# A streamed weight unit fetched by two transfers of 64 partitions in place of one of 128

## The chip, the cores and the metric

The kernel runs on one core of one Trainium2 chip. The metric is the device time of one execution in microseconds, as the median of several runs. The profile is one more execution, recorded by the hardware profiler.

## The reference

The reference adds three things to each other: the input `x`, a two-layer network with GELU on the normalised input (`B`), and an attention layer that carries a memory from segment to segment (`A`). Only `A` matters for the change:

```python
xn = layernorm(x)                      # 2048 x 1024
mem = mem0                             # 8 x 1024
for s in range(64):                    # segments of 32 rows, strictly one after the other
    h = concatenate([mem, xn[32*s : 32*s + 32]])          # 40 x 1024
    q, k, v = h @ Wq, h @ Wk, h @ Wv                      # 32 heads of 128: each W is 1024 x 4096
    p = softmax(where(mask, q @ k.T / sqrt(128), -1e9))   # per head, 40 x 40
    o = (p @ v) @ Wo                                      # Wo is 4096 x 1024
    mem = o[:8];  outs.append(o[8:])
return x + concatenate(outs) + gelu(xn @ w1 + b1) @ w2 + b2
```

The memory that segment s leaves is an input of segment s + 1, so the 64 segments can't be computed side by side. Each of them needs all four weight matrices, 32 MB in bf16[...].

## The kernel before, in words

**Two stages.** The first stage (lines 270 to 548) computes the layer norm and the GELU network for all rows in four groups, and puts rows to be added later into DRAM. The second (from line 555) is the loop over the 64 segments.

**Units, resident and streamed.** The four matrices are cut into 64 units of 512 KB, each a tile of 128 partitions by 2,048 bf16 values, 4 KB in a partition. `ORDER` (line 67) is the order in which a segment uses them: K, Q, K, Q, V, V, then the 16 units of the output product. Forty-six units are fetched once and stay in SBUF for the whole loop. The 18 others, marked `S` in the hand-written string `PLACED` (line 68), are *streamed*: they are fetched again in every segment from copies that stand contiguously in DRAM (`copies`, line 192, named `Wc_...` in the profile). One of the 18 (`IN_PSUM`) is kept in PSUM after the first segment and is brought back by VectorE copies (lines 224 to 226), so later segments fetch 17. One of these (`HALF`) has half of its columns resident and is fetched as 256 KB.

**The ring.** `start_stream` (line 220) begins the fetch of the next streamed unit into one of six buffers (`STREAM_BUFS`), in rotation, from the SyncE queue (line 229). It is called six times at the end of the first stage (line 516) and after that by `unit_done` (line 608), each time a streamed unit has been used. So a new fetch waits until TensorE has done with the unit that held the same buffer six units ago. All fetches are issued by SyncE in program order; a waiting one holds up those behind it. In the segment loop SyncE issues next to nothing else; the small loads and stores of rows go through GpSimd's queue.

**Who uses the units.** `half_pass` (line 668) goes over the eight units of half of K, Q or V and calls `product` (line 644), which runs four 32-column-wide matmuls of 512 values at line 650. `o_product` (line 820) does the same for the output product, at line 829. Both take streamed tiles from a queue in the order in which they were begun (`unit_tile`, line 596). Small steps of attention (`scores`, `sums`, `values`) are placed between units.

**Completion.** The framework gives the transfers of the hardware queue eight semaphores in rotation. A transfer that is given a semaphore waits for the transfer that had it before, the eighth back.

Of the kernel before, what the change touches and what calls it, by code (L numbers as in the profile page):

```python
# [78 lines left out]
def kernel(  # L79
# [16 lines left out]
    nc = tc.nc  # L96
# [42 lines left out]
    def slab(place):  # L139
        if place in low:  # L140
            return low[place]
        return slabs.tile([P, 2048], BF16, name="u", tag=place)
# [9 lines left out]
    for j in range(4):  # L152
# [10 lines left out]
        out=m, in_=m, pattern=[[1, NX]], compare_op=ALU.is_ge, fill=0.0, base=0, channel_multiplier=-1,  # L163
    )
    for half in range(2):
        m = mask_left[0:SEG, :, 8 - 8 * half:16 - 8 * half]
        nc.gpsimd.affine_select(
            out=m, in_=m, pattern=[[-8, GRP], [0, 8]], compare_op=ALU.is_ge, fill=0.0, base=0, channel_multiplier=1,
        )
        nc.gpsimd.affine_select(  # L170
            out=m, in_=m, pattern=[[8, GRP], [1 if half else 0, 8]], compare_op=ALU.is_ge, fill=0.0,
# [13 lines left out]
    for k in range(7):  # L185
# [6 lines left out]
    copies = {  # L192
        unit: dram.tile([P, 1024 if unit == HALF else 2048], BF16, name="Wc_" + "_".join(map(str, unit)))[:, :]
        for unit in reversed(ORDER) if IS_STREAMED[unit]
    }
# [20 lines left out]
    streams = [unit for _ in range(NSEG) for unit in ORDER if IS_STREAMED[unit]]  # L216
    stream_tiles = deque()
    started = 0

    def start_stream():  # L220
        nonlocal started
        if started < len(streams):
            t = slab(RING[started % STREAM_BUFS])
            if streams[started] == IN_PSUM and "kept" in nxt:
                for b in range(2):
                    nc.vector.tensor_copy(out=t[:, 1024 * b:1024 * b + 1024], in_=nxt["kept"][:, b, :])  # L226
            else:
                c0 = 1024 if streams[started] == HALF else 0
                nc.sync.dma_start(out=t[:, c0:2048], in_=copies[streams[started]])
            stream_tiles.append(t)  # L230
            started += 1

# [38 lines left out]
    with tc.tile_pool(name="ma", bufs=2) as ma, tc.tile_pool(name="mps", bufs=6, space=PSUM) as mps:  # L271
# [28 lines left out]
        for j in range(4):  # L300
            nc.sync.dma_start(
                out=o_sb[32 * j + NX:32 * j + 32, 0:8, :],
                in_=mem0[:, 256 * j:256 * j + 256].rearrange("m (h e) -> m h e", h=8),
# [6 lines left out]
        for i in range(14):  # L310
            t = slab(f"w2_{i}")[:, :].rearrange("p (c d) -> p c d", d=DM)
# [120 lines left out]
        for tg in range(4):  # L432
# [14 lines left out]
            for fb in range(FC):  # L447
                ps = mps.tile([P, 512], F32, name="ps")
                for kt in range(KT):
# [9 lines left out]
                    out=xb[:, :], in_=ps[:, :], func=ACT.Identity, bias=b1col[:, fb:fb + 1], scale=1.0  # L459
# [4 lines left out]
                    out=u[:, :], in0=u[:, :], scalar1=0.044715, scalar2=1.0, op0=ALU.mult, op1=ALU.add  # L464
# [7 lines left out]
            if tg == 0:  # L472
                for nb in range(2):
                    cs = slice(nb * 512, nb * 512 + 512)
                    ps = mps.tile([P, 512], F32, name="ps")
# [3 lines left out]
            if not last:  # L479
# [10 lines left out]
                for t in range(4):  # L490
# [3 lines left out]
                    for nb in range(2):  # L494
                        cs = slice(nb * 512, (nb + 1) * 512)
                        ps = mps.tile([P, 512], F32, name="ps")
# [16 lines left out]
            else:  # L513


                for _ in range(STREAM_BUFS):
                    start_stream()
# [37 lines left out]
    with tc.tile_pool(name="late", bufs=1) as late, \  # L555
# [40 lines left out]
        def unit_tile(unit):  # L596
            if IS_STREAMED[unit]:
                return stream_tiles.popleft()[:, :]
            return res_tiles[unit]
# [8 lines left out]
        def unit_done(unit):  # L608

            if IS_STREAMED[unit]:  # L610
                start_stream()
                if late_units:
                    fetch_late(late_units.popleft())
                for _ in range(2 if len(small) > 8 else 1):
                    if small:
                        small.popleft()()
# [9 lines left out]
        for s in range(NSEG):  # L626
# [269 lines left out]
            for n, unit in enumerate(O_UNITS):  # L896
                t = unit_tile(unit)
# [26 lines left out]
            for w, r in enumerate(tiles):  # L924
                nc.vector.tensor_tensor(out=r[:, :], in0=psX[:, 256 * w:256 * w + 256], in1=r[:, :], op=ALU.add)  # L925
                if left_o and not final:

                    for b in range(2):
                        c0 = 256 * (2 * b + w)
# [71 lines left out]
```

## Time and profile before

| What | Value |
|---|---|
| median of 3 runs | 1974.53 us (1971.98 to 1985.32) |
| profiled span | 1971.6 us |
| PE busy | 1771.2 us, 90% |
| VectorE, ScalarE, GpSimd busy | 855.1, 591.9, 287.0 us |
| data moved by DMA | 644.36 MB, mean 327 GB/s |
| streamed transfers (line 229) | 1,025 of 512 KB, 64 of 256 KB |
| first streamed fetch | at 363.4 us |
| last streamed fetch begun | at 1958.2 us |

The page has a row of 40 slices of the span for each engine, with its busy share in tenths, and below them the share for the core's 16 DMA engines and their rate in GB/s. A stretch is the same for a window of one's own choice: length, busy time of each engine with its number of instructions, then the granted TensorE clock, the DMA share and the rate. A line of the waits reads: engine, line of the waiting instruction, what it waited for, then the sum in us, the number of waits and the longest one. A piece of the chain reads: start, length, and what ran or was waited for. PE busy time has to be read with care here: the ends of matmuls are modelled[...].

### The profile page before, as it was taken

How to read it: one execution, taken by the hardware profiler on the slowest of the kernel's cores; microseconds unless marked ns; L12 is line 12 of the kernel's file. 1: busy time of each engine (PE TensorE's matmuls, PEld its weight loads, DVE VectorE, ACT ScalarE, POOL GpSimd, SP SyncE). 2: the span in 40 equal slices, each digit the busy share in tenths (PEclk: the TensorE clock that was granted, in tenths of full speed). 3: DMA queues.
4: the chain of work that ended last, by engine and by line, in shares of the span. 5: the costliest groups of instructions: out<-in, count | busy, mean ns of one | idle time of the engine just before them, and what ended most of it. 6: DMA issues, size and time to landing. Idle time of an engine off the chain costs nothing.

```text
span 1971.6 us, 77130 instructions
## 1 busy us (share of the span) xinstructions
PE 1771.2 (90%) x34271; PEld 962.3 (49%) x34291; DVE 855.1 (43%) x2233; ACT 591.9 (30%) x1349; POOL 287.0 (15%) x557
## 2 busy tenths in 40 slices
PE   6999999999888989898889888989888988998887
PEld 3444444445444445555444546555455454554544
DVE  6657575414344334344434443434344443434432
ACT  4434343302222223222223222222222322222222
POOL 0000000002331111111112111211111111111112
PEclk9999999999999999999999999999999999999999
DMA  9821212689999999999999999999999999999998
GB/s 335 264 56 42 57 41 56 247 305 390 376 363 383 368 372 384 364 379 369 382 371 390 380 392 367 388 377 385 358 386 371 391 379 379 374 389 377 388 367 331
DMA packets 225850, 644.36 MB, mean 327 GB/s; under 512 B 48123, under 2 KB 61739, under 8 KB 225500
## 3 DMA queue, kind: packets, MB, share of 16 engines
q1 hardware_dynamic: 207228, 619.26, 83.7%
q0 software_dynamic: 16928, 18.77, 2.9%
q8 instruction: 268, 4.39, 0.9%
q10 hardware_dynamic: 1360, 1.39, 0.2%
q14 instruction: 66, 0.54, 0.1%
HBM read 625.08 MB, written 31.26 MB: 333 GB/s over the span
## 4 chain that ended last, share of the span: by engine, by line
PE 63%; DMA 26%; issue 5%; DVE 4%; ACT 1%; POOL 1%; ACTq 0%; POOLq 0%; DVEq 0%
PE acc L650 28%; DMA u<-Wc_O 12%; PE acc L829 10%; PE ps L450 10%; PE ps L498 7%; DMA u<-Wc_V 7%; DMA u<-Wc_Q 4%; DMA out_dram<-res 2%; PE ps L531 2%; PE mixed L803 1%; DVE b_oL L707 1%; PE mixed L753 1%; PE acc L803 1%; POOL out_dram L963 1%; PE pT L531 1%
## 5 line engine op out<-in xcount | busy, mean ns | idle before, releaser
L650 PE MATMUL acc<-u,hr 128*32 128x512 bf16 x11520 | 791.9, 382 | 33.3 <-DMA u<-Wc_V 12.1
L650 PEld LDWEIGHTS <-hr 128*32 128x32 bf16 x12288 | 351.6, 97 | 313.9 <-issue 72.5
L650 PE MATMUL acc<-u,hrL 128*32 128x512 bf16 x2880 | 260.7, 389 | 6.1 <-issue 5.9
L829 PE MATMUL acc<-u,d_oL 128*32 128x256 bf16 (+1 forms) x3330 | 184.2, 292 | 20.4 <-issue 11.1
L450 PE MATMUL ps<-u 128*128 128x512 bf16 x896 | 196.2, 382 | 2.6 <-ACT u L346 2.6
L829 PE MATMUL acc<-u,b_oL 128*32 128x256 bf16 (+1 forms) x1776 | 127.1, 304 | 51.3 <-DMA u<-Wc_O 32.1
L829 PEld LDWEIGHTS <-b_oL 128*32 128x32 bf16 (+1 forms) x3552 | 115.5, 102 | 109.6 <-issue 76.2
L498 PE MATMUL ps<-u 128*128 128x512 bf16 x657 | 146.2, 379 | 0.8
L450 PEld LDWEIGHTS <-u 128*128 128x128 bf16 x896 | 88.2, 98 | 109.4 <-issue 5.5
L829 PEld LDWEIGHTS <-d_oL 128*32 128x32 bf16 (+1 forms) x3552 | 100.6, 98 | 62.0 <-issue 34.4
L650 PEld LDWEIGHTS <-hrL 128*32 128x32 bf16 x3072 | 91.8, 98 | 63.7 <-issue 24.4
L829 PE MATMUL acc<-W_O,b_oL 128*32 128x256 bf16 (+1 forms) x1776 | 112.8, 302 | 7.3 <-issue 7.3
L879 POOL DMA_DIRECT2D res<-hr_d x64 | 35.8, 559 | 559.7 <-DVE d_oL L816 304.1
L707 DVE STREAM_TRANSPOSE kT<-kT 128x512 bf16<-128x512 bf16 x64 | 45.5, 711 | 164.4 <-ACT kT L693 164.4
L226 DVE COPY u<-kept 128x1024 bf16<-128x1024 bf16 x126 | 81.2, 687 | 77.7 <-PE acc L829 60.0
L803 PEld LDWEIGHTS <-v 32*128 32x128 bf16 x2048 | 63.6, 91 | 97.8 <-issue 74.5
L707 DVE STREAM_TRANSPOSE b_oL<-b_oL 128x512 bf16<-128x512 bf16 x128 | 90.6, 708 | 46.8 <-ACT b_oL L693 46.8
L693 ACT CAST kT<-acc 128x512 bf16<-128x512 f32 x64 | 37.5, 586 | 222.0 <-PE acc L650 222.0
L498 PEld LDWEIGHTS <-u 128*128 128x128 bf16 x672 | 65.3, 98 | 77.3 <-DVE g_u L466 0.4
L693 ACT CAST b_oL<-acc 128x512 bf16<-128x512 f32 x128 | 75.4, 589 | 80.2 <-PE acc L650 80.2
L963 POOL DMA_DIRECT2D out_dram<-res x124 | 63.4, 517 | 246.5 <-DVE res L925 245.9
L816 DVE CAST b_oL<-acc 128x160 bf16<-128x160 f32 x128 | 41.6, 325 | 131.7 <-PE acc L809 131.7
(139 smaller groups left out, 2221.8 us busy)
## 6 DMA issues: line engine op xcount, KB each, us to landing
u<-Wc_O SPq DMA_DIRECT2D x320, 512.0 KB
u<-Wc_K SPq DMA_DIRECT2D x256, 512.0 KB
u<-Wc_V SPq DMA_DIRECT2D x256, 512.0 KB
u<-Wc_Q SPq DMA_DIRECT2D x193, 512.0 KB
u<-Wc_O SPq DMA_DIRECT2D x64, 256.0 KB
u<-in_B_w_dram SPq DMA_DIRECT2D x16, 448.0 KB
u<-in_B_w_dram SPq DMA_DIRECT2D x14, 512.0 KB
u<-in_A_Wq_dram SPq DMA_DIRECT2D x12, 512.0 KB
```

The costliest lines, as they stand in the source:

```text
L226: nc.vector.tensor_copy(out=t[:, 1024 * b:1024 * b + 1024], in_=nxt["kept"][:, b, :])
L450: nc.tensor.matmul(ps[:, :].rearrange("p (s t) -> p s t", t=SEG), lhsT=w1_sb[fb // 14 * 8 + kt][:, (fb % 14) * P:(fb % 14 + 1) * P], rhs=x ...
L498: nc.tensor.matmul(ps[:, :], lhsT=gts[fc // 4][:, fc % 4, t * P:(t + 1) * P], rhs=w2_sb[fc // 2][:, fc % 2, cs], start=(fc == 0), stop=(fc ...
L531: nc.tensor.matmul(pss[2 * t + nb][:, :], lhsT=gts[fc // 4][:, fc % 4, t * P:(t + 1) * P], rhs=w2_sb[fc // 2][:, fc % 2, nb * 512:nb * 512 ...
L650: nc.tensor.matmul(o, lhsT=lhs[:, i, :], rhs=m, start=(i == seq[0]), stop=(i == seq[-1]), tile_position=(0, 32 * j),)
L693: cp(out=out, in_=ps.rearrange("p (h e) -> p h e", e=32))
L707: nc.vector.transpose(out=home, in_=home)
L803: nc.tensor.matmul(oV[b][:, c, :], lhsT=V[q, c * P:(c + 1) * P], rhs=prA[q, c, :], start=(c == 0), stop=False, skip_group_check=True, tile ...
L816: cp(out=outs[u][:, hs, NL * slot:NL * slot + 40], in_=oV[b])
L829: nc.tensor.matmul(acc[r:r + n // 8, 0:n], lhsT=lhs[:, 4 * (i % 4) + 2 * u + k, :], rhs=w_k[:, n * jq:n * jq + n], start=(unit == O_UNITS[ ...
L879: nc.gpsimd.dma_start(out=st["res"][:, :], in_=hr_d[s + 1, :, 256:512])
L963: nc.gpsimd.dma_start(out=out_flat[rows, 256 * j:256 * j + 256], in_=res[32 * j:32 * j + NX, :])
```

## The change

Each streamed fetch is begun as two transfers, one for partitions 0 to 63 and one for partitions 64 to 127, one behind the other on the same queue, in place of one for all 128. Bytes, source, destination and order stay as they are. Its purpose is to have smaller transfers, each with a completion of its own, for the same unit. The other fetches (resident units, rows, the first stage's weights) are untouched.

```diff
             else:
                 c0 = 1024 if streams[started] == HALF else 0
-                nc.sync.dma_start(out=t[:, c0:2048], in_=copies[streams[started]])
+                for b in range(2):
+                    ps = slice(64 * b, 64 * b + 64)
+                    nc.sync.dma_start(out=t[ps, c0:2048], in_=copies[streams[started]][ps, :])
             stream_tiles.append(t)
             started += 1
```

## The prediction

> **What bounds the kernel now.** I read the page from the top, then the table of stretches, the waits of the transfer queue, the chain in a window, and the compiled instruction order of both kernels. The page first, because it misleads:
>
> ```profile
> PE 1771.2 (90%) x34271; PEld 962.3 (49%) x34291; DVE 855.1 (43%) x2233; ACT 591.9 (30%) x1349; POOL 287.0 (15%) x557
> ...
> DMA  9821212689999999999999999999999999999998
> GB/s 335 264 56 42 57 41 56 247 305 390 376 363 383 368 372 384 364 379 369 382 371 390 380 392 367 388 377 385 358 386 371 391 379 379 374 389 377 388 367 331
> ...
> q1 hardware_dynamic: 207228, 619.26, 83.7%
> ...
> PE 63%; DMA 26%; issue 5%; DVE 4%; ACT 1%; POOL 1%; ACTq 0%; POOLq 0%; DVEq 0%
> PE acc L650 28%; DMA u<-Wc_O 12%; PE acc L829 10%; PE ps L450 10%; PE ps L498 7%; DMA u<-Wc_V 7%; DMA u<-Wc_Q 4%; DMA out_dram<-res 2%; PE ps L531 2%; PE mixed L803 1%; DVE b_oL L707 1%; PE mixed L753 1%; PE acc L803 1%; POOL out_dram L963 1%; PE pT L531 1%
> ```
>
> TensorE looks like the bound at 90% and 63% of the chain. But the DMA row sits at 9 (90% or more) in every slice from the tenth to the last but one. The stretches say how full it really is; the last columns are clock, DMA share and GB/s:
>
> ```profile
> 440.00:465.00 25.00, 22.33 (x560) 13.08 (x560) 11.29 (x28) 5.59 (x15) 1.28 (x2) 0.97 1.03 402
> ...
> 600.00:800.00 200.00, 176.20 (x4272) 99.94 (x4262) 81.12 (x216) 56.41 (x144) 32.14 (x61) 0.98 1.00 378
> 800.00:1000.00 200.00, 176.70 (x4156) 99.46 (x4159) 78.80 (x209) 54.74 (x138) 31.47 (x59) 0.97 0.99 374
> 1000.00:1200.00 200.00, 178.03 (x4332) 100.06 (x4324) 81.49 (x217) 57.78 (x147) 32.12 (x60) 1.00 1.01 382
> ```
>
> From 440 us on the 16 DMA engines are never idle. Weighting the stretches from 440 to 1960 us by length gives 575 MB in 1520 us, 378 GB/s. So the recurrent stage, 77% of the time, is transfer-bound: its length is bytes over rate, and nothing in the rows hides a lost GB/s. The chain shows the other face of it, waits for streamed units that last far longer than one unit's own transfer:
>
> ```profile
> 1035.40 7.49 DMA u<-Wc_O
> ...
> 1051.38 6.85 DMA u<-Wc_V
> ...
> 1079.07 6.76 DMA u<-Wc_O
> ```
>
> One 512 KB unit takes 0.5243 MB / 0.378 = 1.39 us of all 16 engines. Issue to use of about 7 us is five units queued one behind the other. The queue's own waits show why no more are queued:
>
> ```profile
> SPq L229 <- PE acc L650: 583.8, 687, 3.4
> SPq L229 <- PE acc L829: 226.7, 238, 3.7
> ```
>
> SyncE mostly waits for TensorE to give back one of six buffers, which TensorE does as soon as it has used the unit that has just landed.
>
> [...]
>
> **The change, part by part.**
>
> *Issues.* The compiled order has 1,403 SyncE rows before and 2,492 after: 1,089 more, one for each streamed transfer, and no row more on any other engine. An issue takes 320 ns on SyncE (the median of L229), so 1,089 x 0.32 = 348 us of SyncE over 1,520 us, 17 x 0.32 = 5.4 us per segment of some 24 us. SyncE waits 584 + 227 us for TensorE alone, so this hides in its waits. Cost on the path: 0.
>
> *Waits on TensorE.* The first matmul of a streamed unit waited on one transfer; now its weight load waits on one half and the matmul on the other, still without extra instructions. Queued behind them is the whole of TensorE, but both halves are begun back to back and it needs both, so it waits for the later, as before. Cost: 0 beyond the transfers' own lengthening.
>
> *Transfers in flight.* In the compiled order each SyncE transfer waits for the eighth before it (eight rotating semaphores). That was eight units, more than the six buffers; with halves it is four units. So the half-transfer of a new unit waits for the landing of the fourth unit before it, and every later unit is queued behind that wait on SyncE. Four units are 5.6 us of work for the engines; after the wait ends three units, 4.2 us, are still queued. The rows show no turnaround near that: an issue is 0.32 us, and GpSimd's 64 KB loads land 5 to 6 us after issue, but on engines that are never idle. Between 0 and 1 us per segment (64 us); I take 0.
>
> *Bytes and packets.* Same bytes; a row of 4 KB stays a row of 4 KB. No cost.
>
> *Completions.* Twice as many. Nothing in the trace prices one.[...]
>
> *Ports.* This is the large term.[...] Streamed bytes after 440 us: 1,016 of 512 KB and 64 of 256 KB, 549.4 MB; the other 25.6 MB of the stage stay at 378 GB/s, 68 us. At 231: 549.4/0.231 = 2,378 + 68 = 2,446 us; plus 440 us ahead of the stage and 12 us after it, 2,898 us.[...] I take 231.[...]
>
> **The rivals.**
> A. *In step[...]*, 2,898 us (2,750 to 3,160). For: [...]a stage with no slack.[...]
> B. *Drifted apart*, 2,511 us (2,300 to 2,750).[...]
> C. *No port limit, only dearer completions*, 1,972 + 205 = 2,177 us at the upper end, 2,070 in the middle.[...]
> D. *Hidden*: halves run as wholes, 1,972 us.
> E. *Faster*[...] Against: [...]the engines are never idle now.
>
> **How the numbers follow.** A 0.52, B 0.20, C 0.17, D 0.07, E 0.04. The forecast is A, 2,898 us. The range leaves out D, E, the lower part of C and what lies above 3,160 us: from 2,100 to 3,160, some 8 in 10. Slower by over 1%: A, B and nearly all of C, 0.88; within 1%: D and the little of C at its lower end, 0.08; faster 0.04.
>
> **What would show it.** A right: the stretches after 440 us show about 235 GB/s in all (575 MB in 2,446 us) at a DMA share still near 1.0, TensorE's busy time falls to some 55 to 65%, its waits for the streamed units become the largest in the list, and the DMA share of the chain passes 60%. B: the same at about 280 GB/s. C: 335 to 365 GB/s. The first 360 us must be the same in all. Wrong altogether if the stage keeps 370 GB/s or more. Wrong in the step on transfers in flight if the DMA share falls clearly below 1.0 while SyncE waits on transfers.

## The result, and the profile after

The changed kernel takes 2715.51 us (median of 4 runs, 2704.34 to 2731.86) against 1977.21 us of the kernel before in the same comparison: 1.374 times as long, 95% interval 1.365 to 1.382. The prediction was 2,898 us, slower, in a range of 2,100 to 3,160.

The page of the changed kernel, lines as shown of before:

```profile
PE 2039.7 (75%) x34271; PEld 965.2 (36%) x34291; DVE 859.8 (32%) x2233; ACT 585.9 (22%) x1349; POOL 286.9 (11%) x557
...
DMA  9512179999999999999999999999999999999999
GB/s 323 148 42 63 42 235 267 241 238 242 262 255 253 256 269 263 278 272 273 255 248 261 272 247 252 256 250 259 252 270 255 243 253 254 249 256 249 256 242 241
...
q1 hardware_dynamic: 224652, 619.33, 89.4%
...
DMA 79%; PE 18%; SPq 1%; DVE 1%; issue 0%; ACT 0%; POOL 0%; POOLq 0%; ACTq 0%
DMA u<-Wc_O 23%; DMA u<-Wc_Q 20%; DMA u<-Wc_V 20%; DMA u<-Wc_K 14%; PE ps L452 7%; PE ps L500 5%; PE acc L652 3%; DMA hr<-hr_d 1%; PE ps L533 1%; PE acc L831 1%; SPq L231 1%; DMA W_O<-in_A_Wo_dram 1%; DMA u<-in_A_Wo_dram 0%; PE pT L345 0%; DMA u<-in_A_Wv_dram 0%
```

The DMA row is as full as before and the rate under it has fallen from some 375 to some 255 GB/s. The same bytes pass (619.33 MB on the hardware queue against 619.26), in 17,424 packets more, all of them of four bytes (39,007 on this queue, 21,583 before), which is 16 for each of the 1,089 added transfers. The chain has turned over: 79% of it is now waiting for transfers, 26% before. Lines of the changed kernel stand two further down (line 231 for 229, 652 for 650, 831 for 829).

The stretches of the changed kernel, columns as before (the last three are clock, DMA share and GB/s):

```profile
0.00:363.00 363.00, 344.25 (x1660) 160.04 (x1676) 228.91 (x574) 153.09 (x248) 11.92 (x44) 1.00 0.38 118
...
600.00:800.00 200.00, 143.13 (x2828) 68.06 (x2820) 54.94 (x146) 38.31 (x98) 28.03 (x52) 0.85 1.04 253
800.00:1000.00 200.00, 144.91 (x2856) 68.80 (x2860) 55.35 (x145) 37.34 (x95) 22.95 (x43) 0.87 1.03 260
1000.00:1200.00 200.00, 148.06 (x3080) 73.04 (x3076) 58.08 (x151) 39.14 (x100) 22.29 (x42) 0.86 1.03 268
```

The first 363 us are untouched. From 440 to 2690 us the same 575 MB take 2,250 us, 256 GB/s, where they took 1,520: the 730 us that the kernel has lost are all in this stage, and the DMA engines stay full in it (a share above 1 comes of packets that overlap in the record: for 43% of the time from 600 to 1600 us more than 16 are under way). TensorE's granted clock is lower too, 0.85 to 0.87 in the three stretches shown for 0.97 to 1.00, but TensorE waits for data (619 us, below).

Pieces of the chain, and then the waits of the transfer queue and of TensorE:

```profile
1500.93 7.43 DMA u<-Wc_Q
...
1508.38 7.19 DMA u<-Wc_V
...
1515.59 7.51 DMA u<-Wc_O
```

```profile
SPq L231 <- DMA u<-Wc_O: 329.4, 542, 2.2
SPq L231 <- DMA u<-Wc_V: 254.5, 468, 1.9
SPq L231 <- DMA u<-Wc_K: 238.3, 413, 2.2
SPq L231 <- DMA u<-Wc_Q: 175.1, 332, 2.0
```

```profile
PE acc L831 <- DMA u<-Wc_O: 267.9, 260, 3.0
PE acc L652 <- DMA u<-Wc_V: 163.1, 220, 3.2
PE acc L652 <- DMA u<-Wc_Q: 122.9, 156, 3.2
PE acc L652 <- DMA u<-Wc_K: 65.1, 70, 2.6
```

Between these waits for transfers the chain holds next to no work. SyncE now waits mostly for a transfer to land, the eighth half back, and no longer for TensorE to give back a buffer: 997 us in the four lines. TensorE waits 619 us for streamed units; before, the largest such line was this one:

```profile
PE acc L829 <- DMA u<-Wc_O: 41.2, 77, 1.6
```

Which packets are longer? The trace holds every DMA packet with its size and time. The table is worked out from these records, for packets of 4,096 B (one partition's row of a unit) on the hardware queues, from 590 us on to 70 us before the end. The runs below the first two are explained in the next section.

```
run                                  rows      mean ns   quarter / median / three quarters
before                               112,907   171       159 / 159 / 159
changed                              119,132   258       232 / 260 / 284
even and odd partitions              114,646   178       159 / 159 / 159
lower, upper, upper, lower           119,556   278       251 / 287 / 309
two queues (both)                    118,738   264       about 236 / 265 / 292
lower half only                       55,940   299       275 / 314 / 325
quarters 0, 32, 64, 96               120,760   263       233 / 273 / 300
quarters 0, 64, 32, 96               119,988   229       159 / 224 / 262
```

Before, 77% of the rows took 159 ns and 93% at most 170. After, 3% took 159 ns, and 96% lie between this and its double, 318 ns. The records name neither the engine nor the partition of a row, so they don't show what makes it longer; the experiments vary which partitions a transfer holds.

### The profile page after: what moved, and what is told of

Same layout as the page of the kernel before. It is cut to its first block, busy times and chain, and to the rows that moved or that the text cites. A ratio compares the mean times of both kernels' runs of the same rounds, so it can differ in the third digit from the quotient of the medians.

```text
span 2702.6 us, 78400 instructions
## 1 busy us (share of the span) xinstructions
PE 2039.7 (75%) x34271; PEld 965.2 (36%) x34291; DVE 859.8 (32%) x2233; ACT 585.9 (22%) x1349; POOL 286.9 (11%) x557
## 3 DMA queue, kind: packets, MB, share of 16 engines
q1 hardware_dynamic: 224652, 619.33, 89.4%
## 4 chain that ended last, share of the span: by engine, by line
DMA 79%; PE 18%; SPq 1%; DVE 1%; issue 0%; ACT 0%; POOL 0%; POOLq 0%; ACTq 0%
DMA u<-Wc_O 23%; DMA u<-Wc_Q 20%; DMA u<-Wc_V 20%; DMA u<-Wc_K 14%; PE ps L452 7%; PE ps L500 5%; PE acc L652 3%; DMA hr<-hr_d 1%; PE ps L533 1%; PE acc L831 1%; SPq L231 1%; DMA W_O<-in_A_Wo_dram 1%; DMA u<-in_A_Wo_dram 0%; PE pT L345 0%; DMA u<-in_A_Wv_dram 0%
## 5 line engine op out<-in xcount | busy, mean ns | idle before, releaser
L652 PE MATMUL acc<-u,hr 128*32 128x512 bf16 x11520 | 881.6, 401 | 358.8 <-DMA u<-Wc_V 163.1
L652 PEld LDWEIGHTS <-hr 128*32 128x32 bf16 x12288 | 322.4, 101 | 792.4 <-DMA u<-Wc_V 179.1
L831 PE MATMUL acc<-u,b_oL 128*32 128x256 bf16 (+1 forms) x1776 | 147.0, 371 | 217.2 <-DMA u<-Wc_O 215.5
L652 PE MATMUL acc<-u,hrL 128*32 128x512 bf16 x2880 | 298.8, 466 | 0.0
L831 PE MATMUL acc<-u,d_oL 128*32 128x256 bf16 (+1 forms) x3330 | 226.4, 341 | 54.3 <-DMA u<-Wc_O 52.4
L831 PEld LDWEIGHTS <-d_oL 128*32 128x32 bf16 (+1 forms) x3552 | 110.6, 113 | 129.9 <-DMA u<-Wc_O 57.6
L831 PE MATMUL acc<-W_O,b_oL 128*32 128x256 bf16 (+1 forms) x1776 | 135.6, 370 | 1.1 <-issue 1.1
L910 ACT CAST d_oL<-acc 128x256 bf16<-128x256 f32 x63 | 23.4, 372 | 477.5 <-PE acc L831 477.5
L452 PEld LDWEIGHTS <-u 128*128 128x128 bf16 x896 | 87.9, 98 | 108.7 <-issue 4.0
L790 ACT ACTIVATE mixed<-mixed 128x160 f32<-128x160 f32 x128 | 36.9, 288 | 308.3 <-PE mixed L786 308.3
```

What stands on the lines that cost most here:

```text
L452: nc.tensor.matmul(ps[:, :].rearrange("p (s t) -> p s t", t=SEG), lhsT=w1_sb[fb // 14 * 8 + kt][:, (fb % 14) * P:(fb % 14 + 1) * P], rhs=x ...
L652: nc.tensor.matmul(o, lhsT=lhs[:, i, :], rhs=m, start=(i == seq[0]), stop=(i == seq[-1]), tile_position=(0, 32 * j),)
L790: nc.scalar.activation(out=dA, in_=dA, func=ACT.Ln)
L831: nc.tensor.matmul(acc[r:r + n // 8, 0:n], lhsT=lhs[:, 4 * (i % 4) + 2 * u + k, :], rhs=w_k[:, n * jq:n * jq + n], start=(unit == O_UNITS[ ...
```

## The experiments

The theory, which the expectations call *ports*, is that the side counts: rows of the lower or of the upper 64 partitions take longer when they come together. *With drift* means that they come together for only a part of the time. No trace had shown this. Its rivals are the other things that the edit doubles or halves: completions and issues (twice as many), and units in flight (at most four in place of six, since a transfer waits for the eighth before it; counted by the rows that had landed at each issue, the traces show up to 5 units before and up to 7 halves after). A second question is how much the order of the sides counts, for the changed kernel was faster than the forecast.

### Halves that span all partitions

```diff
-                    ps = slice(64 * b, 64 * b + 64)
-                    nc.sync.dma_start(out=t[ps, c0:2048], in_=copies[streams[started]][ps, :])
+                    nc.sync.dma_start(out=t[b::2, c0:2048], in_=copies[streams[started]][b::2, :])
```

> Each streamed unit in two transfers of 64 partitions as in the changed kernel, but the even and the odd partitions in place of the lower and the upper 64. Same number of transfers, same 4 KB rows, same issues, completions and number in flight; each transfer now spreads over partitions 0 to 127. Ports[...]: clearly faster than 2,715 us[...]. Completions, issues or fewer units in flight: 2,700 us, as in the changed kernel.

Measured: 2101.69 us, 1.064 times before (1.058 to 1.069).

```diff
-                for b in range(2):
-                    ps = slice(64 * b, 64 * b + 64)
-                    nc.sync.dma_start(out=t[ps, c0:2048], in_=copies[streams[started]][ps, :])
+                n = (2048 - c0) // 2
+                for b in range(2):
+                    nc.sync.dma_start(
+                        out=t[:, c0 + n * b:c0 + n * b + n], in_=copies[streams[started]][:, n * b:n * b + n],
+                    )
```

> Each streamed unit in two transfers of all 128 partitions and half of the columns. Same number, size and order of transfers as in the changed kernel, but rows of 2 KB[...]. Ports: 1,975 to 2,080 us (rows of 2 KB cost 87 ns each in the trace of before, two of them 174 against 171 for one of 4 KB). Completions, issues or fewer units in flight: 2,700 us.

Measured: 2038.19 us, 1.027 times (1.022 to 1.032). A stretch of the even and odd partitions, then one of the columns:

```profile
1000.00:1400.00 400.00, 342.06 (x7944) 182.65 (x7940) 150.28 (x402) 105.97 (x269) 59.87 (x112) 0.96 0.97 351
```

```profile
1000.00:1400.00 400.00, 354.75 (x8081) 191.15 (x8080) 152.10 (x405) 106.56 (x272) 61.30 (x115) 0.97 1.01 359
```

Both make 2,178 transfers as the changed kernel does, with the same bytes in each and the same limit of eight in flight, and the first also has the same rows of 4 KB. They run at 351 and 359 GB/s. Of the 738 us only some 120 (even and odd) and 56 us (columns) remain, so more than 600 us come not from the number of transfers but from which partitions each one holds. With even and odd partitions all three quartiles of the row time are back at 159 ns; in that run the DMA share falls to 0.97, a loss that the next experiment looks at.

One thing these runs can't tell apart: in every run row p of a unit's copy in DRAM goes to partition p, so a half by side is also one stretch of the copy. Whether the limit lies where the rows are written or where they are read was not tested.

### As many transfers, whole units

```diff
-                for b in range(2):
-                    ps = slice(64 * b, 64 * b + 64)
-                    nc.sync.dma_start(out=t[ps, c0:2048], in_=copies[streams[started]][ps, :])
+                nc.sync.dma_start(out=t[:, c0:2048], in_=copies[streams[started]])
+                nc.sync.dma_start(out=tiny[started % 8][:, :], in_=bd[0:16, 0:16])
```

The line that makes the eight small DRAM tiles `tiny` is left out here.

> Each streamed unit in one transfer of 128 partitions as before, followed by a transfer of 512 bytes (16 partitions of 32 bytes of a constant tile to a DRAM scratch[...], read by nobody). As many transfers, issues, completions and rotating semaphores as in the changed kernel, so four units in flight[...]. Ports: 1,975 to 2,010 us. Completions, issues or fewer units in flight: 2,600 us or more.

Measured: 2096.92 us, 1.059 times (1.056 to 1.063). Far from 2,600, but also outside what was expected of ports alone: 115 us for tiny transfers. To tell units in flight from issues and completions, every second tiny transfer was left out:

```diff
-                nc.sync.dma_start(out=tiny[started % 8][:, :], in_=bd[0:16, 0:16])
+                if started % 2:
+                    nc.sync.dma_start(out=tiny[started // 2 % 8][:, :], in_=bd[0:16, 0:16])
```

> Whole units, with the 512-byte transfer after every second unit only: 5.3 units in flight in place of 4 (before: the six buffers). If the 115 us that the tiny transfer after every unit cost come from fewer units in flight: most of it is gone, 1,980 to 2,010 us. If they come from issues and completions: half is left, 2,035 to 2,045 us.

Measured: 1987.93 us, 1.005 times (1.003 to 1.007). A stretch and two waits with a tiny transfer after every unit, then the same with every second one:

```profile
1000.00:1400.00 400.00, 342.79 (x7927) 190.61 (x7915) 147.94 (x395) 104.02 (x266) 61.84 (x116) 0.96 0.98 354
```

```profile
SPq L230 <- DMA u<-Wc_O: 148.0, 220, 2.5
...
SPq L230 <- PE acc L652: 70.8, 159, 1.7
```

```profile
1000.00:1400.00 400.00, 354.71 (x8572) 202.38 (x8564) 161.31 (x429) 113.04 (x287) 64.67 (x122) 0.99 1.01 380
```

```profile
SPq L230 <- PE acc L653: 302.2, 422, 3.8
...
SPq L230 <- DMA u<-Wc_O: 111.5, 152, 2.3
```

Nearly half of the tiny transfers are still there (513 of 1,089), but 9 us are left of 115, not some 54. This speaks for the number in flight: with four units SyncE waits mostly for landings and some engines run dry now and then (share 0.98, 354 GB/s), with 5.3 it waits mostly for TensorE again, as before, and they don't (share 1.01, 380 GB/s). The number alone doesn't settle it, though: the columns have four units in flight too, keep the engines at a share of 1.01 and lose 56 us. What makes that difference was not tested. The four-byte packets, of which each added transfer of the changed kernel has 16, are short: they have a median of 9 ns in both of these runs, and a mean of 15 in the changed kernel.

### How much the order of the sides counts

First the order of the halves, so that 128 rows on a side, one behind the other in the queue, take the place of 64:

```diff
-                for b in range(2):
+                for b in ((0, 1), (1, 0))[started % 2]:
```

> As the changed kernel, but every second unit begins with its upper half (lower, upper, upper, lower). All counts as in the changed kernel. Ports with drift[...]:[...] mean time of a 4 KB row near 290 ns in place of 258, 2,800 to 2,950 us. Ports without drift, completions, issues or units in flight: 2,715 us, unchanged.

Measured: 2890.49 us, 1.461 times (1.453 to 1.469), and 278 ns for a row where 290 had been expected. Nothing differs from the changed kernel but the order of the halves in every second unit, and it costs another 175 us. Then one side alone, in buffers that keep the rest of their values, and as its control the same bytes over all partitions (the lines that keep the six buffers for the whole loop are left out):

```diff
-                for b in range(2):
-                    ps = slice(64 * b, 64 * b + 64)
-                    nc.sync.dma_start(out=t[ps, c0:2048], in_=copies[streams[started]][ps, :])
+                np_ = P if started < STREAM_BUFS else 64
+                nc.sync.dma_start(out=t[0:np_, c0:2048], in_=copies[streams[started]][0:np_, :])
```

> After the first six fetches only the lower 64 partitions of a streamed unit are fetched; the upper half keeps the values of the first six units. Half of the streamed bytes, each transfer on the same side. Ports:[...] a 4 KB row takes 318 ns, twice the 159 of before, with little spread; 206 GB/s, 275 MB in 1,333 us, with the other 68 and 452 us 1,850 us, and the DMA share stays near 1. Without a port limit: as the run with half of the columns.

```diff
-                for b in range(2):
-                    ps = slice(64 * b, 64 * b + 64)
-                    nc.sync.dma_start(out=t[ps, c0:2048], in_=copies[streams[started]][ps, :])
+                n = 2048 - c0 if started < STREAM_BUFS else (2048 - c0) // 2
+                nc.sync.dma_start(out=t[:, c0:c0 + n], in_=copies[streams[started]][:, 0:n])
```

> After the first six fetches only half of the columns of a streamed unit are fetched, for all 128 partitions; the other half keeps older values. The same 275 MB as with the lower half only[...]. The stage is then bound by the engines, not by transfers: DMA share well below 0.8, 1,500 to 1,800 us, faster than with the lower half only.

Measured: 1900.37 us with the lower half only (0.960, 0.956 to 0.963), 1770.65 us with half of the columns (0.894, 0.891 to 0.897). A stretch of the first and one of the second:

```profile
1000.00:1400.00 400.00, 368.97 (x8880) 213.98 (x8880) 168.48 (x449) 117.68 (x300) 68.72 (x129) 0.99 0.96 206
```

```profile
1000.00:1400.00 400.00, 390.92 (x9758) 229.28 (x9752) 183.92 (x491) 129.27 (x327) 74.05 (x140) 1.00 0.73 226
```

The control moves 226 GB/s with the DMA engines idle a quarter of the time (share 0.73): the compute engines are its bound (TensorE is busy for 391 of these 400 us), at 1,771 us, which is an estimate of what the kernel before would come to if it didn't have to wait for transfers. The lower half alone, at fewer bytes per us, keeps the DMA engines at 0.96. So 64 partitions on one side move 206 GB/s here, some 215 if the engines were full (an estimate: 206/0.96). The expected 1,850 us and 318 ns for every row came out as 1,900 us and 314 ns in the median, but a fifth of the rows took less than 250 ns.

Next, the two halves from two queues:

```diff
-                for b in range(2):
+                for b, eng in enumerate((nc.sync, nc.scalar)):
                     ps = slice(64 * b, 64 * b + 64)
-                    nc.sync.dma_start(out=t[ps, c0:2048], in_=copies[streams[started]][ps, :])
+                    eng.dma_start(out=t[ps, c0:2048], in_=copies[streams[started]][ps, :])
```

> The halves of the changed kernel, the lower begun by SyncE and the upper by ScalarE. The rows, bytes and halves are the same, but they stand in two queues[...]. Ports with drift:[...] mean time of a 4 KB row 165 to 240 ns, 2,050 to 2,450 us, some of it for ScalarE's waits. If engines stay exactly in step: 2,715 us or more.

Measured: 2750.71 us, 1.389 times (1.384 to 1.394): no gain at all, and the expectation of 2,050 to 2,450 us was wrong. It rested on a supposition that no trace had shown: that two queues are served a row at a time in turn, so that the stretch on one side would be one row. A stretch, and two waits that ScalarE's new task brought:

```profile
1000.00:1400.00 400.00, 289.21 (x5687) 142.00 (x5675) 109.50 (x287) 72.99 (x190) 43.98 (x83) 0.84 1.03 253
```

```profile
ACT d_oL L910 <- DMA u<-Wc_Q: 292.6, 45, 9.0
ACT mixed L790 <- DMA u<-Wc_V: 225.6, 57, 5.7
```

ScalarE's waits are long, but the engines are full (1.03) at 253 GB/s, and a row takes 264 ns, no less than with one queue (258). The packet records name the queue. Of the rows under way at one moment, take the share that belongs to SyncE's queue (worked out from these records, every 20 ns). If the queues took turns with every row, this share would turn around after one row. But after 0.26 us, one row, it is still much as it was (correlation 0.71), after 0.52 us somewhat (0.42), and only near 0.9 us is nothing left of it. Both queues nearly always had rows waiting. So the queues did not take turns by the row in this run: the supposition failed, and the stretches on one side didn't become one row long.

Last, quarters, which shorten the stretch on one side with one queue. Four transfers for a unit leave only two units in flight, so the two orders are to be compared with each other:

```diff
-                for b in range(2):
-                    ps = slice(64 * b, 64 * b + 64)
+                for b in (0, 1, 2, 3):
+                    ps = slice(32 * b, 32 * b + 32)
                     nc.sync.dma_start(out=t[ps, c0:2048], in_=copies[streams[started]][ps, :])
```

> Each streamed unit in four transfers of 32 partitions in the order 0, 32, 64, 96:[...] two units in flight. Ports with drift: the same mean time of a 4 KB row as in the changed kernel, 258 ns, plus what fewer units in flight cost: 2,720 to 2,950 us.

```diff
-                for b in (0, 1, 2, 3):
+                for b in (0, 2, 1, 3):
```

> The same four transfers of 32 partitions in the order 0, 64, 32, 96[...]. All counts as in the run with the order 0, 32, 64, 96. If[...] the length of a stretch on one side sets what that saves: clearly faster than that run, mean row 200 to 240 ns, 2,350 to 2,650 us. If[...] engines take whole transfers in step: the same as that run within 2%.

Measured: 2948.69 us in the first order (1.488 times, 1.472 to 1.504) and 2803.07 in the second (1.415, 1.399 to 1.430). A stretch of each:

```profile
1000.00:1400.00 400.00, 276.34 (x5280) 136.17 (x5278) 101.30 (x265) 67.74 (x173) 41.59 (x78) 0.83 0.95 235
```

```profile
1000.00:1400.00 400.00, 291.45 (x5577) 143.93 (x5572) 105.54 (x278) 72.83 (x186) 40.18 (x75) 0.81 0.88 247
```

The row came down from 263 to 229 ns, as expected of 32 rows on a side in place of 64, but 2,803 us lie far above the 2,350 to 2,650 that had been expected. The engines ran dry more often (share 0.88 for 0.95). With two units in flight in both orders, what grew is SyncE's part: it makes four issues for a unit, with medians of up to 419 ns. The chains of the two runs in the same order:

```profile
DMA 58%; PE 24%; SPq 14%; issue 3%; DVE 0%; ACT 0%; POOL 0%; POOLq 0%; ACTq 0%
```

```profile
DMA 39%; PE 31%; SPq 23%; issue 5%; DVE 1%; ACT 0%; POOL 0%; POOLq 0%; ACTq 0%
```

SyncE's issues are 14% and 23% of them, 1% in the changed kernel. Part of the shorter rows may come from the lower share of 0.88 itself; this wasn't tested apart.

## Why the prediction was right or wrong

**The bound: right.** The stage is bytes over rate before and after, and nothing hid the loss. The control run puts a number on the slack there was: with half of the streamed bytes, where transfers are no longer the bound, the kernel still takes 1,771 us.

**Ports: right in kind, mis-sized.** This is the term that the miss comes from. The prediction took 231 GB/s for the streamed bytes. The trace of before, in which every streamed transfer holds 128 partitions, does not show this. Measured: 2,250 us of the stage, less the 68 us of the other bytes, leave 2,182 us for 549.4 MB, 252 GB/s. That is 196 us less than the 2,378 of the sum, and the forecast was 182 us too high. That the side counts is shown: one side alone moved 206 GB/s at a DMA share of 0.96, with 314 ns for a row in the median; even and odd partitions moved 351, with 159. But two sides in turn moved more than one side alone: in all, 256 GB/s against 206, which is 24%. The row times lie mostly between 159 and 318 ns, and they go with the stretch on one side: 278 ns for 128 rows, 258 for 64, and in quarters 229 for 32 against 263 for 64. What makes a row longer is in no record.

So the result lies between the prediction's cases A (2,750 to 3,160) and B (2,300 to 2,750), just inside B's band. That the side counts is common to both: in A the rows of one side come together all of the time, in B for a part of it, and no run shows how the engines stand to each other. That the forecast, made with case A, came within 7% owes something to luck: the rate of the stage lay between those of the two cases.

**Completions: right, and smaller than the bound.** The upper end of 205 us (rival C), which rested on no number of the trace, is out: with the same number of transfers the columns cost 56 us in all, and 513 added small transfers cost 9.

**Transfers in flight: 0 in the sum, with a bound of 64 us that may be too low.** Where rows are fast, four whole units in flight with tiny transfers between them cost 115 us, and most of this went when 5.3 could be in flight; four units by column cost 56. The argument that a queue with three units in it can't run dry does not hold for the first of these; it left out that the next issue also waits for TensorE and stands behind other waits on SyncE, which may be why. In the changed kernel it costs little or nothing, since the slower rows keep the engines full (share 1.03): the value was right for a reason that the prediction didn't give.

**Issues: right at 0, with a wrong duration.** The prediction used 320 ns. The issues of the streamed fetches, before, changed, and with even and odd partitions (fastest, median and slowest in ns, then first and last start):

```profile
L229 SPq DMA_DIRECT2D u<-Wc_O x384: 319/320/1055, 446.2 to 1958.2; - x192
```

```profile
L231 SPq DMA_DIRECT2D u<-Wc_O x768: 444/445/1492, 453.0 to 2689.4; - x192
```

```profile
L230 SPq DMA_DIRECT2D u<-Wc_O x768: 450/547/2154, 447.2 to 2086.5; - x192
```

Two issues of 445 ns for a unit that now takes 2 us remain hidden, and SyncE is 1% of the chain. With even and odd partitions two of 547 ns stand beside some 1.5 us for a unit, and SyncE's issues are 5% of that kernel's chain; this may be why it trails the columns (issues of 320 ns in most) by 63 us, but that wasn't tested apart.

**The signs.** DMA share near 1.0, waits for streamed units on top, and more than 60% of the chain came as foretold; the rate was 256 GB/s, about midway between the 235 of case A and the 280 of case B. TensorE's busy time fell to 75%, not to 55 to 65%: its instructions are recorded as longer (a matmul of line 650 had 382 ns, of line 652 now 401), at a lower clock (0.879 for 0.985).

## What to carry to other kernels

Where transfers are the bound, look at which partitions one transfer holds before looking at how many transfers there are: here, at the same count and size, halves that span the partitions cost 3 to 6%, halves by side 37%. Count how many transfers the rotating semaphores allow in flight before splitting any; here 5.3 whole units were enough, and with four the engines ran dry now and then, though not in every arrangement. Splitting further also adds issues: with quarters these were 14 to 23% of the chain. And a DMA share of 1.0 did not say here that the engines moved what they can (378 GB/s before, 256 after): the time of a single packet told the difference, 159 ns and 260 in the median.

## What the runs showed that was not expected

- Issuing a transfer of 64 partitions took SyncE longer than issuing one of 128: 445 ns against 320 for the lower and upper halves, about 545 for every second partition.
- Two queues from two engines did no better than one: 264 ns a row against 258. The queues did not take turns by the row (correlation 0.71 after one row).
- TensorE's mean granted clock was lower in the kernels in which it was busy less: 0.997 where it was busy 96% of the span (half of the columns), 0.985 at 90% (before), 0.879 at 75% (changed), 0.842 at 72% (quarters in the first order).
